# Attention and expert kernel: two dense blocks' activations ahead of the one-hot rows, first gates on their own, a loaded iota

## The chip, the cores and the metric

The kernel runs on one core of one Trainium2 chip. The metric is the device time of one execution in microseconds, as a median over executions. The engines of the core are called as the profile calls them: PE multiplies matrices (PEld are its weight loads), DVE, ACT and POOL work on vectors, SP issues most of the DMA transfers, and POOL issues the indirect ones. Each engine executes its own instructions in order and waits for the others by semaphores, so an instruction that waits holds up all that stand behind it on its engine. SP's queue is such an engine too.

## What is computed

The output is the input plus two branches, both over the normalized input `xn` (2048 rows, 512 columns):

```python
# attention: 32 heads of 16, one shared key and value head
q = (xn @ wq).reshape(...); k = xn @ wk; v = xn @ wv
p = softmax(q k^T * 16 ** -0.5); a = (p v) @ wo
# experts: 32 heads, each with two sets of 64 scores; 64 x 64 = 4096 experts
s1, s2 = q1 @ k1.T, q2 @ k2.T              # per row and head, 64 scores each
t1, i1 = top2(s1); t2, i2 = top2(s2)
top_s, top_e = top2(t1 + t2, over the 4 pairs)  # index = i1 * 64 + i2
g = softmax(top_s)
act = gelu(xn . u[top_e])                  # tanh form
b = sum over heads and both experts of g * act * v[top_e]
out = x + a + b
```

So each row has 64 experts out of 4096, two per head.

## The kernel before

**Groups and ways.** The 16 row tiles of 128 are four groups of four. For groups 0 and 1 the experts are *gathered*: for each row tile and slot, POOL fetches 128 rows of `u` and `v` by index (L880), DVE forms a dot product (L892, `dot`) and later adds the weighted `v` row to an accumulator (L927, `add`). For groups 2 and 3 they are computed *densely*: all 4096 experts, in 32 blocks of 128, are multiplied with the group's 512 rows, and a matrix of gates, zero nearly everywhere, selects. The sequence `SEQ` is: scores of group 0, two eighths of group 1, group 2 with its dense stage, the rest of group 1, group 3 with its dense stage.

**Attention goes on all the time.** `att_steps` (L1037) is called 280 times. 256 of them put out two key tiles' worth of attention: scores on PE (L318), an exp on ACT (L321, tile `pt`), and the product with the values on PE (`pv`, L332). In the middle of a step `mid` puts out expert work for DVE and ACT; at its end `fill` runs the generator `score_thread` (L998) for as much PE work as a linear plan (`aim`) allows. What the generator yields is the planned PE cost of the piece in us. A yield of `None` ends the filling of this step, so that the next piece comes behind another attention step.

**Lists of later work.** `ON_ACT`, `LAST` and `LATER` hold ACT work for the next `mid` or the one after it; `BEHIND` holds DVE work that is laced into the dots and adds of a `mid`; `STORES` holds DMA issues, run at the start of the next step. How many dots a step may put out is set by `pos`, which grows by 1.7, 2.5 or 1.4 slots per step according to `dense_on` (L1152), and over the last quarter evenly to the end. All engines are scheduled by hand here: the order of the calls is the order on the engines.

**From scores to gates.** `item` (L513) multiplies a row tile with an eighth of the score weights (`psc`, L532), and DVE finds the best values and their indices (MAX8 L542, FIND_INDEX8 L544). After four row tiles `batch` (L561) forms the pairs: two index rows `df1`, `df2` (L628, L629) and, after an exp on ACT that comes two `mid`s later, the gates `dgt` (L632 to L640, among them `gh` at L638). They are written to tiles named `da`. `dense` (L645) then does this:

1. It makes an iota of shape 128x128x16 on POOL (L701) and fetches the first two raw expert blocks (`rw`, 256 KB of `u` and 256 KB of `v` each, L654, two buffers).
2. It transposes the three rows (`ptd`, L711) into `tr`.
3. In 32 rounds of 16 columns it forms one-hot rows on DVE by comparing the iota with `tr` (`oh`, L722 to L725) and multiplies them on PE (`pg`, L749). ACT copies the products to `gst` (L754). Every fourth round two stores of 16 blocks each go to `d_g` in memory, in packets of 256 bytes (L757).
4. Behind the last store `first_gates` (L728) fetches the gate rows of blocks 0 and 1 back (`gy`, L672) and four tiles of `x`.
5. For each block (L788): `split` (L677) makes a high and a low part of `u` and `v` (cast on ACT L684, subtraction on DVE L685); 12 matmuls give the activations (`pact`, L796); square, tanh and products with the gate on ACT and DVE follow (L818 to L825); the result is split again into `wd` (L828, L832); and for two blocks at a time 24 matmuls (`pout`, L780) and four additions (L783) bring them to the accumulator. `fetch_gates` (L666) waits for a free gate tile.

`split` of a block, `fetch` of the block two further on and the fetch of its gates are queued as the loop goes on, so the raw blocks, the gate stores and the gate fetches share one SP queue with attention's loads (`qa`, `ot`, `rc`) and with the loads of partial sums (`fin`, L420) that finished row tiles need on DVE (L433).

Of the kernel before, what the change touches and what calls it, by code (L numbers as in the profile page):

```python
# [54 lines left out]
def tile_kernel(ctx, tc, x, wq, wkv, wo, wqT, kT, uv, ub, vb, out):  # L55
# [17 lines left out]
    d_w = [dram.tile([P, KC, 2, 512], F32, name=f"dw{c}") for c in range(NC)]  # L73
    d_g = dram.tile([NB, P, 512], F32, name="dg")
# [478 lines left out]
    DT = []  # L553
# [7 lines left out]
    def batch(ph, c, b):  # L561
# [52 lines left out]
        if c == 0:  # L614
            DT.clear()
            dense_tiles()
# [14 lines left out]
        def gates():  # L631
# [8 lines left out]
            stt(dgt[:, :, 1, w], gg, GS, gh, op0=OP.mult, op1=OP.subtract)  # L640

# [3 lines left out]
    def dense(DG, after):  # L645

        df1, df2, dgt = DT[:3]
# [12 lines left out]
        def gate_tile(b):  # L660
            if b not in gates:
                gy = late[0].tile([P, 2, 512], F32, name="gy", tag="gy", bufs=3)
                gates[b] = gy
            return gates[b]

        def fetch_gates(b):  # L666
            if b < NB and b not in fetched:
                if formed[0] < b - 2:

                    store(lambda: fetch_gates(b))  # L670
                    return
                nc.sync.dma_start(gate_tile(b)[:, 0, :], d_g[b])  # L672
                fetched.add(b)

        splits, halved = {}, set()

        def split(b):  # L677
            if b < NB:
                if b not in raws:
                    run(STORES)  # L680
                rw = raws.pop(b)
                us, vs = wk_tile(), wk_tile()
                for i, w in enumerate((us, vs)):
                    nc.scalar.copy(w[:, 0, :], rw[:, i, :])  # L684
                    behind(lambda w=w, i=i: nc.vector.tensor_tensor(out=w[:, 1, :], in0=rw[:, i, :], in1=w[:, 0, :],  # L685
                                                                    op=OP.subtract))
                behind(lambda: halved.add(b))
                splits[b] = us, vs
# [11 lines left out]
        io = kt(F16, (P, P, TB))  # L700
        nc.gpsimd.tensor_copy(io, iota_h[:, :, None].to_broadcast([P, P, TB]))  # L701
        fetch(0)
        fetch(1)
        yield None
        tr = kt(F16, (P, 3, 512))
        for n, src in enumerate((df1, df2, dgt)):
            if n == 2:
                yield None
            p = xtile("ptd")
            for j in range(GT):  # L710
                nc.tensor.transpose(p[:, j * P:(j + 1) * P], src[:, j].rearrange("p r s -> p (r s)"), ident)  # L711
            nc.scalar.copy(tr[:, n, :], p)
            yield 0.45
        dense_on[0] = 2
# [3 lines left out]
        def onehot(q):  # L718
            if q < NQ:
# [3 lines left out]
                ob = kt(F16, (P, NB, TB))  # L723
# [4 lines left out]
        def first_gates():  # L728

            fetch_gates(0)  # L730
            fetch_gates(1)
# [6 lines left out]

        onehot(0)
        onehot(1)  # L740
        for q in range(NQ):
# [10 lines left out]
            def copies(pv_=pv_, st=st, ql=ql, t0=t0):  # L752
                for hb in range(2):
                    nc.scalar.copy(st[hb][:, :, ql * TB:(ql + 1) * TB], pv_[:, 16 * hb:16 * hb + 16, :])  # L754
                if ql == 3:
                    for hb in range(2):
                        store(lambda hb=hb: nc.sync.dma_start(  # L757
                            d_g[16 * hb:16 * hb + 16, :, t0:t0 + 64].rearrange("b p t -> p b t"), st[hb]))
# [11 lines left out]
        def sums():  # L770
# [4 lines left out]
            for j in range(GT):  # L775
                p = xtile("pout")
                n = 0
                for wd, vs in ready:
                    for a, c in TERMS:
                        nc.tensor.matmul(p, wd[:, a, j * P:(j + 1) * P], vs[:, c, :], start=n == 0, stop=n == 5)  # L780
# [7 lines left out]
        for b in range(NB):  # L788
            if b not in halved:
                flush()  # L790
            us, vs = splits.pop(b)
            p = xtile("pact")
            n = 0
            for k in range(KC):
                for a, c in TERMS:
                    nc.tensor.matmul(p, us[:, a, k * P:(k + 1) * P], XT[DG][k][:, c, :],  # L796
                                     start=n == 0, stop=n == 11)
                    n += 1
                if k == 0:
                    store(lambda b=b: fetch_gates(b + 1) if b else None)  # L800
                    if b % 2 == 0:
                        later_split(b + 2)
                if k == KC - 1 and b == NB - 1 and after is not None:
                    wp_read(after, range(2))
                if b == NB - 1 and after is not None:
                    load_phase2_xt(SEQ[after][0], k)
                if k < KC - 1:
                    yield 3 * UNIT
            wd = late[0].tile([P, 2, 512], F32R, name="wd", tag="wd", bufs=4)

            if b > 1 and b not in fetched:
                if formed[0] < b - 2:
                    flush()
                run(STORES)
            gy = gate_tile(b) if b < 2 else gates[b]
            gates.pop(b - 1, None)
            g, y = gy[:, 0, :], gy[:, 1, :]
            nc.scalar.activation(y, p, AF.Square, scale=C_CUB ** 0.5)  # L818
            stt(y, y, C_IN, p, op0=OP.add, op1=OP.mult)

            def gated(g=g, p=p):
# [4 lines left out]

            def high(y=y, wd=wd):
                nc.scalar.copy(wd[:, 0, :], y)  # L828
                behind(lambda: low(y, wd))
# [429 lines left out]
```

## Time and profile before

| | us |
|---|---|
| median of 3 runs | 2010.13 |
| lowest and highest | 2004.77, 2011.43 |
| profiled execution | 2014.99 |
| its span in the trace | 2013.3 |
| PE busy, granted clock over the span | 1883.9, 0.967 |
| last `psc` of group 2 ends, first `pg` begins | 613.1, 635.4 |
| last `pg` of group 2 ends, first `pout` begins | 760.2, 800.6 |
| last `psc` of group 3 ends, first `pg` begins | 1455.4, 1476.9 |
| last `pg` of group 3 ends, first `pout` begins | 1577.8, 1645.5 |

All stage times are from the trace's timeline, counted from the start of the span. A row of the timeline is: start, length, engine, line, operation, output and inputs by the program's names, count; in brackets the idle time of the engine before it and what ended it. SPq rows are the times in which SP issues a transfer, not the transfer itself. The granted clock (PEclk) is the share of full speed at which PE was clocked; at 0.6 its matmuls take longer, while they still count as busy.

### The profile page before, as it was taken

To read this page: it belongs to the slowest core of one execution; us is meant where nothing else is said; L and a number is where in the kernel's file an instruction comes from. 1 tells how busy PE (TensorE), PEld (TensorE's weight loads), DVE (VectorE), ACT (ScalarE), POOL (GpSimd) and SP (SyncE) were. 2 spreads that over 40 slices of the span, in tenths; PEclk is the share of its full clock that TensorE was granted. 3 is DMA by queue.
4 is the path that set the end of the run, shared out by engine and by line. 5 is a ranking of instruction groups with operands and counts; after the bars stand their busy time and mean duration, and the time that the engine had idled before them with its cause. 6 is when DMAs were issued, how large, how long until landed. Compare 5 with 4: busy or idle time off the path is not lost.

```text
span 2013.3 us, 34723 instructions
## 1 busy us (share of the span) xinstructions
PE 1883.9 (94%) x10990; PEld 1004.4 (50%) x10990; DVE 1683.2 (84%) x6713; ACT 1291.2 (64%) x1804; POOL 573.2 (28%) x542
## 2 busy tenths in 40 slices
PE   6869989899998997999999999999979789999997
PEld 4634444455554443555555445555545345555552
DVE  7536778889999867999999779999999668999993
ACT  2236556655556787778777565555568567788873
POOL 2202223222223223334344222222223333333320
PEclk9989999999998998999999999999989899999999
DMA  7856778787764769788889868776659877888761
GB/s 264 297 191 227 266 246 273 269 285 254 241 226 129 224 194 298 241 281 263 276 293 319 324 236 257 262 259 221 205 139 248 275 253 262 260 277 259 264 209 63
DMA packets 239882, 494.79 MB, mean 246 GB/s; under 512 B 93380, under 2 KB 93380, under 8 KB 239692
## 3 DMA queue, kind: packets, MB, share of 16 engines
q0 software_dynamic: 73728, 268.47, 40.3%
q1 hardware_dynamic: 163960, 222.44, 33.7%
q10 hardware_dynamic: 2004, 1.61, 0.3%
q8 instruction: 88, 1.44, 0.3%
q14 instruction: 102, 0.84, 0.1%
HBM read 429.51 MB, written 57.64 MB: 242 GB/s over the span
## 4 chain that ended last, share of the span: by engine, by line
PE 58%; DVE 25%; DMA 5%; ACT 2%; issue 2%; SPq 1%; ACTq 0%; DVEq 0%
PE pv L332 16%; PE sc L318 12%; PE psc L532 9%; PE pout L780 9%; PE pact L796 8%; DVE i L544 6%; DVE xa L927 4%; DVE m L542 4%; DVE g L892 4%; DMA dg<-gst 2%; DVE oh L722 2%; PE pg L749 2%; PE pwo L427 1%; ACT pt L321 1%; PE pw L487 1%
## 5 line engine op out<-in xcount | busy, mean ns | idle before, releaser
L321 ACT ACTIVATE pt<-sc 128x1024 f32<-128x1024 f32 x1024 | 993.5, 1025 | 495.6 <-PE sc L318 436.7
L880 POOL DMA_INDIRECT g<-in_uv_dram,idx x512 | 556.4, 1087 | 1368.7 <-DVE xa L927 701.0
L332 PE MATMUL pv<-pt,vaug 128*32 128x512 f32 x4096 | 517.0, 623 | 0.0
L318 PE MATMUL sc<-qa,kaug 64*128 64x512 f32 x2048 | 392.4, 457 | 17.4 <-ACT pt L321 16.0
L532 PE MATMUL psc<-wk,xt 128*128 128x512 f32 x1536 | 386.3, 401 | 18.8 <-DVE i L544 13.2
L927 DVE SCALAR_TENSOR_TENSOR xa<-g,w,xa 128x512 f32<-128x512 f32 x512 | 371.5, 747 | 0.0
L532 PEld LDWEIGHTS psc<-wk,xt 128*128 128x128 f32 x1536 | 280.5, 189 | 118.8 <-issue 42.3
L892 DVE CUSTOM_DVE_ANT_0 g<-g,xa 128x512 f32<-128x512 f32 x512 | 336.7, 683 | 2.4 <-DMA g<-in_uv_dram,idx 2.2
L318 PEld LDWEIGHTS sc<-qa,kaug 64*128 64x128 f32 x2048 | 159.1, 188 | 340.1 <-ACT pt L321 209.0
L332 PEld LDWEIGHTS pv<-pt,vaug 128*32 128x32 f32 x4096 | 109.7, 112 | 259.8 <-issue 258.2
L796 PE MATMUL pact<-xt,wk 128*128 128x512 f32 x768 | 198.4, 404 | 11.3 <-DVE fin L433 5.4
L780 PE MATMUL pout<-wk,wd 128*128 128x512 f32 x768 | 197.4, 405 | 10.1 <-DVE wd L832 5.8
L544 DVE FIND_INDEX8 i<-m,psc 128x8 uint32<-128x64 f32 x1024 | 206.7, 223 | 0.0
L542 DVE MAX8 m<-psc 128x8 f32<-128x64 f32 x1024 | 146.6, 216 | 43.5 <-PE psc L532 36.3
L796 PEld LDWEIGHTS pact<-xt,wk 128*128 128x128 f32 x768 | 140.9, 190 | 62.3 <-issue 18.0
L780 PEld LDWEIGHTS pout<-wk,wd 128*128 128x128 f32 x768 | 141.9, 190 | 58.5 <-DVE wd L832 7.1
L783 DVE TENSOR_TENSOR da<-da,pout 128x512 f32<-128x512 f32 x128 | 83.1, 682 | 9.0 <-PE pout L780 8.6
L915 DVE SCALAR_TENSOR_TENSOR w<-gth,ga 128x4 f32<-128x4 f32 x128 | 20.4, 159 | 83.2 <-ACT gth L908 82.9
L685 DVE TENSOR_TENSOR wk<-rw,wk 128x512 fp32r<-128x512 f32 x128 | 85.0, 684 | 0.0
L722 DVE TENSOR_TENSOR oh<-oh 128x2048 f16<-128x2048 f16 x64 | 78.1, 1220 | 6.7 <-PE pg L749 6.7
L749 PE MATMUL pg<-oh 128*128 128x32 f16 x1024 | 73.6, 246 | 9.1 <-DVE oh L725 9.0
L749 PEld LDWEIGHTS <-oh 128*128 128x128 f16 x1024 | 69.3, 162 | 20.5 <-issue 12.7
(150 smaller groups left out, 1350.4 us busy)
## 6 DMA issues: line engine op xcount, KB each, us to landing
wk<-dw SPq DMA_DIRECT2D x96, 512.0 KB
wqt<-in_wqT_dram SPq DMA_DIRECT2D x32, 512.0 KB
dw<-wk SPq DMA_DIRECT2D x32, 512.0 KB
rw<-in_ub_dram SPq DMA_DIRECT2D x64, 256.0 KB
rw<-in_vb_dram SPq DMA_DIRECT2D x64, 256.0 KB
dg<-gst SPq DMA_DIRECT2D x32, 512.0 KB
gy<-dg SPq DMA_DIRECT2D x64, 256.0 KB
qa<-dqh SPq DMA_DIRECT2D x128, 64.0 KB
```

Of the source, the lines that this page charges most:

```text
L318: nc.tensor.matmul(p[:, b, :], kaug[o:o + 64, kc * P:(kc + 1) * P], QA[u][o:o + 64, i, :], start=True, stop=True)
L321: nc.scalar.activation(pt, p, AF.Exp, scale=SCALE)
L332: nc.tensor.matmul(PV[u][32 * j:32 * j + 32, :], vaug[:, kc, :], pt[:, b, :], start=kc == 0, stop=kc == 15)
L532: nc.tensor.matmul(p, XT[g][k][:, a, j * P:(j + 1) * P], WC[n_][k][:, bb, :], start=n == 0, stop=n == 11)
L542: nc.vector.max(m8[:, jb, s, :], p[:, s * E:(s + 1) * E])
L544: nc.vector.max_index(i8[:, jb, s, :], m8[:, jb, s, :], p[:, s * E:(s + 1) * E])
L749: nc.tensor.matmul(p[:, i * NB:(i + 1) * NB], oa[:, :, i], ob[:, :, i], start=True, stop=True)
L780: nc.tensor.matmul(p, wd[:, a, j * P:(j + 1) * P], vs[:, c, :], start=n == 0, stop=n == 5)
L796: nc.tensor.matmul(p, us[:, a, k * P:(k + 1) * P], XT[DG][k][:, c, :], start=n == 0, stop=n == 11)
L880: nc.gpsimd.indirect_dma_start(out=gt, out_offset=None, in_=uv, in_offset=bass.IndirectOffsetOnAxis(ap=IDX[ph, c, ti][:, s:s + 1], axis=0))
L892: nc.vector.tensor_tensor_reduce(u, u, XN[TPH * ph + ti], scale=1.0, scalar=0.0, op0=OP.mult, op1=OP.add, accum_out=a[:, i:i + 1])
L927: nc.vector.scalar_tensor_tensor(acc, v, w[:, i:i + 1], acc, op0=OP.mult, op1=OP.add)
```

## The change

- `dense` is started earlier. It yields 0.0 twice before its real work; `score_thread` takes these steps ahead of the last eighth's first and second item, so that the two raw blocks are fetched, and the `u` halves of blocks 0 and 1 split, while the scores still run.
- `first(b)` computes the activations of blocks 0 and 1 and begins their gelu: square and copy on ACT, then on DVE the inner polynomial, later tanh and (tanh + 1) times the activation. Block 0 comes ahead of the transposes, block 1 between the first and the second one-hot set. In the loop over the blocks these two are only multiplied with their gates (`scaled`) and split. Their `v` halves are split during the one-hot rounds; blocks 0 and 1 leave the loop's `pact` work.
- From the third item of the last eighth to the end of the transposes `dense_on` is 3: no new dots, and one add per step.
- The iota is made once at the start by ACT, stored to memory (`dio`, 512 KB) and loaded by SP in each dense stage.
- The last store of each group is cut into blocks 0 to 2, 3 to 15 and 16 to 31; directly behind the first piece the gate rows 0, 1 and 2 and the `x` tiles are fetched. Gate rows up to 3 no longer wait for formed blocks.
- The small one-hot operand lives in one tile of three slots instead of tiles of its own. The first products (`sums`) are taken at block 4, and some points where the filling ended (`yield None`) are gone or moved.

```diff
@@ zero_m
+        io = gtile(F16, (P, P, 16))
+        nc.scalar.copy(io, iota_h[:, :, None].to_broadcast([P, P, 16]))
+        nc.sync.dma_start(d_io, io)
@@ batch: gates
+            if c == NC - 1:
+                gated_all.append(True)
@@ dense
+        def half_split(b, i):
+            rw, w = raws[b], wk_tile()
+            nc.scalar.copy(w[:, 0, :], rw[:, i, :])
+            behind(lambda: nc.vector.tensor_tensor(out=w[:, 1, :], in0=rw[:, i, :], in1=w[:, 0, :], op=OP.subtract))
+            return w
...
-        io = kt(F16, (P, P, TB))
-        nc.gpsimd.tensor_copy(io, iota_h[:, :, None].to_broadcast([P, P, TB]))
         fetch(0)
         fetch(1)
-        yield None
-        tr = kt(F16, (P, 3, 512))
-        for n, src in enumerate((df1, df2, dgt)):
-            if n == 2:
-                yield None
...
+        yield 0.0
+        early = []
+        on_act(lambda: early.extend(half_split(b, 0) for b in range(2)))
+        yield 0.0
...
+        def first(b):
+            p = xtile("pact")
+            for k in activations(b, early[b], p):
+                if k < KC - 1:
+                    yield 3 * UNIT
+            g, y = gate_rows(b), hh[:, b, :]
+            nc.scalar.activation(y, p, AF.Square, scale=C_CUB ** 0.5)
+            nc.scalar.copy(g, p)
+            nc.vector.scalar_tensor_tensor(y, y, C_IN, p, op0=OP.add, op1=OP.mult)
+
+            def go():
+                nc.scalar.activation(y, y, AF.Tanh)
+                behind(lambda: nc.vector.scalar_tensor_tensor(y, y, 1.0, g, op0=OP.add, op1=OP.mult))
+
+            LATER.append(go)
+            yield 3 * UNIT
...
+        io = kt(F16, (P, P, TB))
+        nc.sync.dma_start(io, d_io)
+        tr = kt(F16, (P, 3, 512))
+        hh = kt(F32, (P, 2, 512))
+        yield from first(0)
+        for n in range(2):
+            spread(n)
             yield 0.45
+        while not gated_all:
+            yield None
+        spread(2)
+        yield 0.45
...
-            fetch_gates(0)
-            fetch_gates(1)
+            for b in range(3):
+                fetch_gates(b)
...
         onehot(0)
+        yield from first(1)
         onehot(1)
...
-                    for hb in range(2):
-                        store(lambda hb=hb: nc.sync.dma_start(
-                            d_g[16 * hb:16 * hb + 16, :, t0:t0 + 64].rearrange("b p t -> p b t"), st[hb]))
-                    if t0 == 448:
-                        store(first_gates)
+                    cut = (0, 3, 16, NB) if t0 == 448 else (0, 16, NB)
+                    for b0, b1 in zip(cut, cut[1:]):
+                        store(lambda b0=b0, b1=b1: nc.sync.dma_start(
+                            d_g[b0:b1, :, t0:t0 + 64].rearrange("b p t -> p b t"),
+                            st[b0 // 16][:, b0 % 16:b0 % 16 + b1 - b0, :]))
+                        if b0 == 0 and t0 == 448:
+                            store(first_gates)
...
-                later_split(q - NQ + 2)
+            if q in (NQ - 6, NQ - 2, NQ - 1):
+                later_split((NQ - 6, NQ - 2, NQ - 1).index(q))
@@ dense, loop over the blocks
+            def scaled(y=y, g=g):
+                stt(y, g, 1.0 / GS, y, op0=OP.mult, op1=OP.mult)
...
+            else:
+                LAST.append(lambda scaled=scaled, high=high: (behind(scaled), on_act(high)))
@@ score_thread
+            dn = None
+            if ph >= NSP and c == NC - 1:
+                dn = dense(ph, n + 1 if n + 1 < len(SEQ) else None)
+                yield next(dn)
             for ti in range(TPH):
+                if dn and ti == 1:
+                    yield next(dn)
+                if dn and ti == 2:
+                    dense_on[0] = 3
...
-                yield from dense(ph, n + 1 if n + 1 < len(SEQ) else None)
+                yield from dn
@@ steps
-                pos += 2.1 if len(IDX) < NC * TPH else (1.7, 2.5, 1.4)[dense_on[0]]
+                pos += 2.1 if len(IDX) < NC * TPH else (1.7, 2.5, 1.4, 0.0)[dense_on[0]]
...
+                if dense_on[0] == 3:
+                    sums = min(sums, 1)
```

More of the change, by code (lines that the diff above doesn't have):

```diff
@@ L615, in batch @@
             DT.clear()
+            gated_all.clear()
             dense_tiles()
@@ L680, in split @@
                     run(STORES)
[L681 to L686, printed above, removed]
+                us = half_split(b, 0) if b > 1 else None
+                splits[b] = us, half_split(b, 1)
                 behind(lambda: halved.add(b))
-                splits[b] = us, vs
+                raws.pop(b)
         def later_split(b):
@@ L788, in dense @@
         for b in range(NB):
[L789 to L808, printed above, removed]
@@ L816, in dense, with gated @@
+            vs = splits.pop(b)[1]
+            gy = gates[b]
             gates.pop(b - 1, None)
[L817 to L821, printed above, removed]
+            g, y = (gy[:, 0, :], gy[:, 1, :]) if b > 1 else (gy[:, b, :], hh[:, b, :])
+            def gated(g=g, p=None):
                 stt(g, g, 1.0 / GS, p, op0=OP.mult, op1=OP.mult)
```

95 lines of the change are left out of this document (61 added, 34 removed).

## The prediction

> **What bounds the kernel now.** First the busy shares on the page:
>
> ```profile
> PE 1883.9 (94%) x10990; PEld 1004.4 (50%) x10990; DVE 1683.2 (84%) x6713; ACT 1291.2 (64%) x1804; POOL 573.2 (28%) x542
> ```
>
> PE (TensorE) sets the time. From 820 to 1100 us it is busy 279.4 of 280 us, from 1660 to 1960 us 299.7 of 300, so there only less PE work could help. What can be won lies where PE stands still or its granted clock falls. Windows of 5 us show where (columns: window, length, busy us of PE, PEld, DVE, ACT, POOL with counts, granted clock, DMA share, GB/s):
>
> ```profile
> 620.00:625.00 5.00, 2.21 (x20) 1.15 (x12) 4.66 (x32) 0.59 (x1) 0.00 (x0) 1.00 0.12 26
> 625.00:630.00 5.00, 3.56 (x16) 1.17 (x20) 4.86 (x17) 4.94 (x8) 1.88 (x2) 0.60 0.46 120
> 785.00:790.00 5.00, 2.22 (x9) 1.26 (x8) 1.36 (x3) 0.62 (x1) 1.87 (x2) 0.98 1.02 398
> 790.00:795.00 5.00, 1.87 (x5) 1.16 (x4) 3.60 (x6) 3.46 (x5) 1.14 (x1) 0.50 0.96 351
> 1460.00:1465.00 5.00, 0.00 (x0) 0.00 (x0) 4.96 (x48) 1.46 (x2) 0.00 (x0) 0.72 0.01 2
> 1600.00:1605.00 5.00, 0.10 (x1) 0.10 (x1) 0.84 (x2) 0.00 (x0) 0.00 (x0) 0.72 0.77 257
> ```
>
> There are two holes in each dense group (groups 2 and 3): A, between the last scores and the first one-hot rows (DVE is full, PE waits), and B, between the last one-hot product and the first `pout` (the DMA share is near 1). The timeline tells what ends the waits:
>
> ```profile
> 1467.47 1.97 PE L711 MATMUL ptd<-ident,da 128*128 128x128 f32 x8 [8.81 <-DVE da L628]
> ...
> 1452.16 2.54 DVE L638 TENSOR_SCALAR gh<-gd 128x32 f16<-128x32 f32 x1
> 1452.75 1.90 POOL L701 COPY oh<-iota_h 128x2048 f16<-128x2048 f16 x1
> ...
> 764.53 8.32 SPq L757 DMA_DIRECT2D dg<-gst  x2
> 777.67 0.81 SPq L672 DMA_DIRECT2D gy<-dg  x2
> 780.72 0.43 SPq L654 DMA_DIRECT2D rw<-in_ub_dram  x1
> 788.70 0.62 ACT L684 CAST wk<-rw 128x512 fp32r<-128x512 f32 x1 [4.46 <-DMA rw<-in_ub_dram]
> 793.37 2.08 PE L796 MATMUL pact<-xt,wk 128*128 128x512 f32 x4 [3.13 <-DVE wk L685]
> ...
> 1604.16 0.69 DVE L433 TENSOR_TENSOR fin<-fin,pwo 128x512 f32<-128x512 f32 x1 [12.45 <-DMA fin<-dpart]
> ...
> 771.30 3.04 PE L796 MATMUL pact<-xt,wk 128*128 128x512 f32 x12
> ```
>
> In A, PE waits for the last batch of indices, which stands behind expert dots and adds on DVE. In B of group 2 the last two stores of the gate rows hold the SP queue 13.1 us (764.53 to 777.67); the first gates, and behind them the raw block that ACT needs next, come after. In B of group 3 the `fin` loads stand in the same queue, and DVE waits 12.45 us for one.
>
> To compare the orders of the two programs I price PE work at full clock: an attention step (8 scores, 16 `pv`) 3.24 us, twelve `pact` matmuls 3.0, sixteen `pg` 1.1, four `ptd` 0.6, eight `pwo` records 3.6, all from steady stretches. What a stretch takes above that is its excess:
> - last `psc` to first `pg`: group 2 22.3 us for 11.5 of work (excess 10.8); group 3 21.4 for 8.2 (13.2).
> - first to last `pg`: 124.8 for 111.7 (13.1); 101.0 for 87.4 (13.6).
> - last `pg` to first `pout`: 40.4 for 28.1 (12.3, and 2.4 right behind it); 67.7 for 52.3 (15.4, and 3.9 behind it).
>
> In all 84.7 us, the most that this change could touch.
>
> **The change part by part.**
>
> *Two activations in hole A.* Per group 24 `pact` matmuls (6.0 us) move from B to A, with two squares and tanhs (0.60 and 0.64 us), four more DVE operations (0.68) and one added ACT copy per block (0.6, hidden: ACT is 64% busy). While `dense_on` is 3 no dots are issued and one add at a time; hardly any DVE work lies between the last batch and the first one-hot.
> Group 2: the changed order puts block 0 and the first transposes behind the first attention step after the scores. PE is free at 616.2, `pact` ends at 619.2. On the way to the last batch DVE trades one dot (0.6) for two subtractions of the split (1.2), so the indices come at 624.1 instead of 623.5; PE waits 4.9 us. Then transposes, attention (about 5 us, the clock being low after the wait), transposes, block 1 and attention end at 638.5. In 25.4 us 17.4 of work is done: excess 8.0, gain 2.8. Bounds: 0 to 6.0 (both blocks wholly inside the hole).
> Group 3: three of the matmuls run before the attention step, nine behind it, until 1461.6. DVE saves the 2.36 us that `gh` L638 took above its 0.18 under the POOL copy, pays 1.2 for the subtractions and trades a dot for an add: indices at 1466.3 instead of 1467.4, PE waits 4.7 instead of 8.8. The gates come 6 us after the indices now; with the dots gone the exp on ACT sets that, some 5 us; block 1 then runs until 1476.6, when the first `pg` begins, and the second one-hot set, which stands behind block 1's DVE step, costs PE 2 us. Gain 13.2 - 7.0 - 2.0 = 4.2; bounds 0 to 9.
>
> *The clock after hole A.* It stays at 0.60 to 0.83 from 625 to 665 us, which makes up most of the 13.1; shorter waits should shorten that. Nothing in the trace shows how much: bounds 0 and 9 for both groups, I take 3, because waits as short as 2.35 and 1.76 us preceded the 0.60.
> [...]
>
> *The iota.* Two POOL copies (1.90) go; what they cost is in group 3 above, in group 2 no DVE row is longer beside it. In their place SP gets two loads of 512 KB; such a load (`wk<-dw`) is common, and it is issued behind the last scores, some 10 us ahead of its use: 0. The first two raw blocks are fetched about three items earlier, past `qa` and `rc` on SP; the DMA share is 0.02 to 0.67 from 600 to 620 us, which hides them: 0, and 2 us (their 1 MB at some 400 GB/s) if it did not.
>
> *Start.* One ACT copy of 128x2048 (by twice the 1.02 us of 128x1024: about 2 us) and a store of 512 KB in a part that is not PE-bound (ACT 3.6 of 10). It stands ahead of the `kaug` issues, in a gap of ACT of 3.3 us: I take +1, bounds -1 to +3.
>
> *First gates by themselves, hole B.* The last store is cut into blocks 0 to 2, 3 to 15 and 16 to 31, with the fetches of gates 0 to 2 and four `x` loads after the first piece. Two stores hold the queue 13.1 us; 3 of 32 blocks are 1.2 us of that, so gates 0 and 1 come some 10 us earlier. But behind the loads SP issues the other 29 blocks (12 us) and only then raw block 4 and gate 3. That order matters: ACT reaches block 4's cast at the second attention step after the last `pg`, because blocks 3 and 4 are split together, and its exps stand behind that cast; DVE meets `gated` of block 3, whose gate row has the same wait.
> Group 2, counted from the last `pg`: attention to 4, block 2 to 7, attention to 10.5, block 3 to 15; then PE waits. Bytes ahead of raw block 4 are those ahead of block 3 before (landed at 28.5), started 3 us sooner, one wait for a store's end shorter, one gate row more: about 25.5. Cast and subtraction: 27. At the low clock that follows, first `pout` at 36, for 18.6 of work: excess 17.4 and some 2 behind it, against 12.3 + 2.4 + 2 before: a loss of 2.5. Bounds: gain 6 (it lands with the first gates), loss 9 (all of 12 us of stores fully in front of it).
> Group 3: four `pwo` groups lie between, so block 3 is wanted only near 30, its raw block lands near 28; the cast waits some 6, and one `fin` load stands behind the stores too. Against stops of 5.4, 3.9 and 1.4 with their low clock I take 13 of excess for 19.3: gain 6; bounds loss 3 to gain 15.
>
> *Dots put off.* About 4 steps at 1.7 slots per group, 13 slots; dot and add stand 0.61 and 0.66 us apart in the timeline, so 17 us of DVE work go to the last quarter, where DVE is busy 274 of 300 us and PE is full. The 26 us of slack take it; I take +1 (bounds 0 to 4), for adds that come late to `pout`. Without that slack it would cost all 17.
>
> **The sum.** -2.8 - 4.2 - 3 + 1 + 2.5 - 6 + 1 = -11.5 us. The profiled execution took 2015.0 us (span 2013.3), so 2003.5; the median shown, 2010.1, is 4.9 below it: about 1999.
>
> **The rivals.**
> 1. *Hole B gives back what hole A won.* For it: the bytes in front of the next raw block are the same. Against: group 3 has other work there. B in both groups at +3 and no clock won: -7 + 6 + 2 = +1, about 2011.
> 2. *The split store becomes the stop: slower.* One mechanism: raw block 4 and gate 3 stand behind 12 us of small-packet stores and the new loads, while ACT and DVE ask for them a block earlier, so ACT, DVE and PE stop together in both groups. For it: the 4.46 us stop at the same cast. Against: `fin` waits go. Price: B +9 and +3, dots +4, against -7 in A: +9, about 2019. It decides once block 4 lands later than some 30 us after the last `pg`.
> 3. *More than I count.* `fin` no longer stops DVE and the clock stays up: B 0 and -15, A -7, clock -6: -28, 1982. For it: 12.45 us is the longest wait there is; against: `fin` is still behind the stores.
> 4. *The holes are only moved* (indices late, blocks wait with them): the 8.81 us wait is DVE's, and the 4.9 us left in group 2 is longer than the 2.35 there now. If only group 3's 4.2 is kept and B is even: 2006.
>
> **How the numbers follow.** Forecast 0.45, rivals 0.17, 0.14, 0.14, 0.10. What can be told from no change is 0.3%, 6 us: below 2004 or above 2016. Faster: 0.35 of the forecast's 0.45, rival 3, 0.03 of rival 1, 0.05 of rival 4: 0.57. Slower: 0.12 of rival 2, 0.03 of rival 1: 0.15. Same: 0.28. The forecast's own range is 1991 to 2008; to hold 8 in 10 it goes to 1981 and 2018, which takes in rival 3 and most of rival 2.
>
> **What would show it.** Hole A: `pact` records before the first `ptd`, waits there of 4 to 5 us instead of 8.81, no POOL copy, `gh` at 0.18. B: `gy<-dg` within 5 us of its store; then a long `rw` wait at ACT's cast and a low clock in group 2, shorter `fin` waits in group 3. Late: PE still full from 1660 on. I am wrong if ACT's wait for raw block 4 is absent or much over 16 us, or if PE shows gaps after 1660.

## The result and the profile after

The changed kernel takes 2021.11 us (median of 20 runs, 2013.13 to 2025.06), the kernel before in the same series 2014.08. The ratio is 1.0031, 95% interval [1.0016, 1.0047]: slower by about what can be told from no change. The forecast was 1999 us and the range ended at 2018. The forecast started from a median of 2010.13 us for the kernel before (3 runs); 20 runs give 2014.08, so 4 of the 22 us between forecast and result belong to that base. The profiled execution took 2022.62 us, its span is 2020.9 against 2013.3.

The busy shares on the page hardly differ from those before:

```profile
PE 1883.2 (93%) x10990; PEld 1002.7 (50%) x10990; DVE 1679.2 (83%) x6713; ACT 1295.8 (64%) x1809; POOL 571.0 (28%) x540
```

So the 7.6 us are places where PE stands. The timeline of hole A in both groups (line numbers are those of the changed kernel from here on: `ptd` L750, `pact` L725, `gh` L643):

```profile
616.04 3.01 PE L725 MATMUL pact<-xt,wk 128*128 128x512 f32 x12
622.95 0.65 PE L750 MATMUL ptd<-ident,da 128*128 128x128 f32 x4 [3.90 <-DVE da L633]
...
1459.12 0.18 DVE L643 TENSOR_SCALAR gh<-gd 128x32 f16<-128x32 f32 x1
1471.38 1.09 PE L750 MATMUL ptd<-ident,da 128*128 128x128 f32 x8 [2.66 <-DVE da L633]
```

The wait of 8.81 us is 2.66 now, `gh` has lost its 2.36 us, and `pact` stands ahead of the transposes. Last `psc` to first `pg` takes 23.7 us for 17.4 of work in group 2 and 18.4 for 14.2 in group 3: excess 6.4 and 4.2, where it was 10.8 and 13.2. Hole A is won.

The same view of hole B in group 2 (SPq rows are issues; the rest are ACT, DVE and PE behind them):

```profile
764.18 0.38 SPq L811 DMA_DIRECT2D dg<-gst  x1
769.71 1.28 SPq L682 DMA_DIRECT2D gy<-dg  x3
771.03 2.39 SPq L787 DMA_DIRECT2D da<-in_x_dram  x4
773.46 6.17 SPq L811 DMA_DIRECT2D dg<-gst  x2
779.73 2.67 SPq L660 DMA_DIRECT2D rw<-in_ub_dram  x1
...
774.96 0.73 PE L725 MATMUL pact<-xt,wk 128*128 128x512 f32 x2 [0.65 <-ACT wk L689]
787.10 0.62 ACT L689 CAST wk<-rw 128x512 fp32r<-128x512 f32 x1 [11.67 <-DMA rw<-in_ub_dram]
789.23 0.69 DVE L877 SCALAR_TENSOR_TENSOR gy<-gy 128x512 f32<-128x512 f32 x1 [8.95 <-ACT gy L894]
790.50 0.68 DVE L690 TENSOR_TENSOR wk<-rw,wk 128x512 fp32r<-128x512 f32 x1
791.24 5.51 PE L725 MATMUL pact<-xt,wk 128*128 128x512 f32 x16 [15.55 <-DVE wk L690]
805.54 4.64 PE L836 MATMUL pout<-wk,wd 128*128 128x512 f32 x10 [3.56 <-DVE wd L888]
```

The first piece is issued in 0.38 us, then SP stands 5.15 us until it has landed, because the gate rows that are fetched next are read from it. Only then come the gates, the `x` tiles, 6.17 us of the other two pieces, and raw block 4. ACT's wait at its cast is 11.67 us (4.46 before), PE's behind it 15.55 (3.13). What PE waits for is not block 4 but block 3: only two of its 12 `pact` matmuls run before the stop (774.96). Its raw rows were cast on ACT right before it (774.30), but the subtraction for it on DVE (790.50) stands behind a product that waits 8.95 us for a tanh (L894), and that tanh stands on ACT behind the cast of block 4.

In group 3 the two later pieces take 8.20 us of the queue, ACT waits 14.2 and PE 16.9. There all pieces also leave later. First the changed kernel, then the kernel before:

```profile
1610.62 0.38 SPq L811 DMA_DIRECT2D dg<-gst  x1
...
1582.68 8.30 SPq L757 DMA_DIRECT2D dg<-gst  x2
```

The first piece is issued 13.1 us after the end of the last `pg` (1610.62 less 1597.53), behind a `fin` store and load and eight `qa` loads; in the kernel before the two stores went out 4.9 us after it (1582.68 less 1577.83), ahead of these. Last `pg` to first `pout`, with the wait right behind it, has an excess of 23.2 us in group 2 (14.7 before) and 22.9 in group 3 (19.3 before).

A third place was not foreseen: the junction, where dense group 2 ends and the scores of group 1 go on. The timeline there:

```profile
1105.01 0.38 SPq L457 DMA_DIRECT2D out_dram<-fin  x1
1119.68 0.32 SPq L424 DMA_DIRECT2D fin<-dpart  x1
1126.63 5.36 SPq L509 DMA_DIRECT2D wk<-dw  x6
...
1124.45 0.69 DVE L456 TENSOR_TENSOR fin<-fin,xa 128x512 f32<-128x512 f32 x1 [5.73 <-DMA fin<-dpart]
1125.79 1.66 PE L836 MATMUL pout<-wk,wd 128*128 128x512 f32 x6 [1.87 <-DVE da L839]
1134.25 0.96 PE L536 MATMUL psc<-wk,xt 128*128 128x512 f32 x3 [2.23 <-DMA wk<-dw]
```

A finished row tile of the gathered groups is stored (`out`), and as there is one `fin` buffer the next `fin` load stands in SP's queue for that store, 14.65 us in the chain of waits. DVE waits 5.73 us for this load, PE for DVE's additions, and the score weights `wk` are issued 4.6 us later than before (1126.63 against 1121.99). PE's longer waits there are 1.87, 2.23 and 1.52 us, where the kernel before has one of 2.12, and from 1136.0 to 1142.7 us the granted clock is 0.50, where it stayed at 1.00 before. To measure it: the eight attention steps from step 128 to step 136 (step n is the exp 4n) hold the same PE work in every version; they take 65.4 us here and 58.6 before. The 3.5 us of added waits and an estimated 3.4 us lost at half clock (half of the 6.7 us at 0.50) make up these 6.8.

### The profile page after: what moved, and what is told of

Same layout as the page of the kernel before. It is cut to its first block, busy times and chain, and to the rows that moved or that the text cites. A ratio compares the mean times of both kernels' runs of the same rounds, so it can differ in the third digit from the quotient of the medians.

```text
span 2020.9 us, 34731 instructions
## 1 busy us (share of the span) xinstructions
PE 1883.2 (93%) x10990; PEld 1002.7 (50%) x10990; DVE 1679.2 (83%) x6713; ACT 1295.8 (64%) x1809; POOL 571.0 (28%) x540
## 4 chain that ended last, share of the span: by engine, by line
PE 61%; DVE 20%; DMA 5%; issue 4%; ACT 2%; POOL 1%; SPq 1%; DVEq 0%; ACTq 0%; POOLq 0%
PE pv L336 17%; PE sc L322 12%; PE psc L536 10%; PE pout L836 8%; PE pact L725 8%; DVE i L548 5%; DVE xa L982 3%; DVE m L546 3%; DVE g L947 3%; PE pg L802 2%; DMA out_dram<-fin 2%; PE pwo L431 1%; ACT pt L325 1%; PE pw L491 1%; DMA wk<-dw 1%
## 5 line engine op out<-in xcount | busy, mean ns | idle before, releaser
L725 PE MATMUL pact<-xt,wk 128*128 128x512 f32 x768 | 198.6, 403 | 18.9 <-DVE wk L690 15.6
L725 PEld LDWEIGHTS pact<-xt,wk 128*128 128x128 f32 x768 | 140.5, 189 | 69.5 <-issue 16.0
L836 PEld LDWEIGHTS pout<-wk,wd 128*128 128x128 f32 x768 | 142.1, 190 | 56.5 <-DVE wd L888 6.8
L689 ACT CAST wk<-rw 128x512 fp32r<-128x512 f32 x128 | 73.9, 628 | 27.3 <-DMA rw<-in_ub_dram 25.9
```

The costliest lines, as they stand in the source:

```text
L836: nc.tensor.matmul(p, wd[0][:, a, j * P:(j + 1) * P], vs[:, c, :], start=n == 0, stop=n == 5)
```

## The experiments

Every version but the kernel before and its three variants has the order of PE's instructions of the changed kernel, so stages can be compared by their length. Hole A is counted from the start of the last `psc` to the start of the first `pg`, hole B from the last `pg` to the first `pout`, in the one profiled execution of each run. Steps 56 to 104 take in the whole dense stage of group 2, steps 180 to 212 that of group 3, each with the same PE work in every version. All lengths in us; the ratio is to the kernel before, run beside it.

| run | median | ratio, 95% interval | A, groups 2, 3 | B, groups 2, 3 | steps 128 to 136 | steps 56 to 104, 180 to 212 |
|---|---|---|---|---|---|---|
| before | 2014.08 | 1 | 22.7, 21.8 | 40.4, 67.7 | 58.6 | 344.6, 241.1 |
| after | 2021.11 | 1.0031 [1.0016, 1.0047] | 24.1, 18.8 | 38.1, 60.9 | 65.4 | 346.3, 241.9 |
| e1_no_defer | 2025.75 | 1.0059 [1.0034, 1.0084] | 28.2, 23.1 | 41.1, 61.5 | 60.4 | 356.1, 243.3 |
| e2_raw_first | 2014.39 | 0.9999 [0.9975, 1.0023] | 25.2, 18.9 | 33.4, 59.0 | 65.1 | 345.1, 241.1 |
| e3_old_store | 2011.84 | 0.9993 [0.997, 1.0015] | 24.9, 19.9 | 38.0, 58.1 | 63.5 | 348.0, 242.1 |
| e4_pool_iota | 2020.25 | 1.0029 [1.0006, 1.0052] | 25.2, 19.7 | 38.5, 62.4 | 65.0 | 349.3, 237.4 |
| e5_pay_back | 2017.94 | 1.0012 [0.9985, 1.0038] | 25.1, 19.7 | 39.1, 60.0 | 64.4 | 349.1, 245.2 |
| e6_old_store_pay_back | 2009.92 | 0.9986 [0.996, 1.0013] | 24.2, 19.7 | 36.0, 56.5 | 64.6 | 343.6, 231.5 |
| e9_old_store_no_defer | 2017.49 | 1.0035 [1.0011, 1.0059] | 26.1, 22.8 | 33.3, 57.8 | 64.1 | 354.6, 239.3 |
| e10_relief | 2005.95 | 0.997 [0.9948, 0.9992] | 25.1, 20.0 | 37.8, 56.5 | 56.7 | 347.3, 240.0 |
| e12_relief_cut | 2012.13 | 1.0003 [0.9981, 1.0026] | 24.9, 19.7 | 38.7, 62.5 | 56.4 | 345.5, 241.7 |
| variants of before: e7_cut_only | 2011.81 | 1.0013 [0.9985, 1.0041] | 21.1, 22.3 | 49.0, 66.8 | 61.2 | 347.2, 246.8 |
| e8_defer_only | 2010.31 | 0.9997 [0.9973, 1.0021] | 18.8, 18.9 | 39.6, 72.1 | 65.3 | 337.7, 241.9 |
| e11_defer_relief | 2006.12 | 0.9976 [0.9948, 1.0004] | 17.9, 18.1 | 37.4, 69.4 | 56.8 | 333.2, 246.5 |

Each run of an experiment has 12 timed executions, which spread by 8 to 21 us. The intervals of two ratios reach some 0.0025 to each side, so one pair alone does not tell apart what differs by less than about 7 us (0.0035 of 2012); the verdicts below rest on pairs that agree and on the stages. Each stage length is from one execution, and not always a typical one: those of e3 and e5 were the slowest of their 12, that of e7 (2026.20 us) the second slowest.

**Without the put-off dots (e1_no_defer).**

```diff
                 if dn and ti == 2:
-                    dense_on[0] = 3
+                    dense_on[0] = 0
```

> The changed kernel without the one step that puts the dots off: during the scores of a dense group's last columns the gathered slots' dots keep their usual rate of 1.7 a step. Theory J (the junction behind dense group 2 costs 7 us because the gathered groups turn over 22 us later there, so the store of fin, its reload and the six wk loads stand one behind the other in SP's queue): the first fin loads lie near 1031 to 1090 again instead of 1053 to 1120, the 14.65 us wait of the next fin load for the store before it falls under 6, the exp count loses its jump of +7 between steps 132 and 136, hole A gives back 2 to 4 us in each group because the dots are in DVE's way again; the time is 2014 to 2018, some 5 us under the changed kernel's 2021. Rival D (the jump follows from the dense group's own later end, whatever the dots do): the jump stays and the time is 2021 to 2025.

The junction behaves as theory J said (60.4 us in place of 65.4), but the time rises to 2025.75, above the ranges of J and D. Hole A gets 4 us longer in both groups: PE waits 4.5 and 2.3 us at the transposes of group 2 where it waited 3.9 and 0.8. Without it the excess of hole A is 10.4 us in group 2 and 8.5 in group 3: the kernel before has 10.8 and 13.2, the changed kernel 6.4 and 4.2. So the put-off is nearly all that the change gains in hole A of group 2 and half of it in group 3, and the junction is what it costs. By the ratios it is worth 0.0028 of the time here and 0.0042 with the old store (e9 against e3). What I took for a harmless side step is its best part.

**The order of the last stores (e2_raw_first, e3_old_store).**

```diff
+        late_store = lambda f: behind(lambda: store(f))
-                        store(lambda b0=b0, b1=b1: nc.sync.dma_start(
+                        (late_store if b0 and t0 == 448 else store)(lambda b0=b0, b1=b1: nc.sync.dma_start(
```

> The changed kernel with the second and third piece of the last gate store put behind the next raw blocks' fetches in SP's queue (in group 2 block 4, in group 3 blocks 3 and 4), nothing else moved. Theory S (hole B's stop is SP's queue: the raw block is late because the two pieces, 6.2 us in group 2 and 8.2 us in group 3, are issued ahead of it): the ACT cast's wait for the raw block falls from 11.7 to 4 to 6 us in group 2 and from 14.2 to 5 to 8 in group 3, the last-pg-to-first-pout stage gets 5 us shorter in group 2 and 5 to 7 in group 3, the time is 2009 to 2013. Rival G (block 3's gates, now stored later, take the raw block's place as the stop): ACT waits less, but DVE waits for gy<-dg by as much, the stage stays within 2 us and the time within 2019 to 2022. Rival L (the packets of the store share the transfer engines with the raw block): the wait falls by under 3 us and the time is 2017 to 2020.

```diff
-                    cut = (0, 3, 16, NB) if t0 == 448 else (0, 16, NB)
+                    cut = (0, 16, NB)
...
-                        if b0 == 0 and t0 == 448:
+                        if b0 == 16 and t0 == 448:
```

> The changed kernel with the last gate store in two pieces again (16 and 16 blocks) and the first three gates and the x loads behind both, as in the kernel before. Theory S (the stop in hole B is at raw block 4, and the cut only serves the first gates, which are not what is late): the raw block is issued at about the same time as in the changed kernel, the ACT wait stays at 10 to 15 us, the first gates come some 6 us later and show in the products of blocks 0 and 1; the time is 2020 to 2024. Rival C (the cut itself, with its extra issue and 3-block packets, is what the hole costs): hole B's stage gets 4 us or more shorter in each group and the time is under 2014.

With the raw block first, ACT's wait falls from 11.67 to 2.90 us (9.7 in group 3), hole B gets 4.7 and 1.9 us shorter, and the time goes from 1.0031 to 0.9999 of before. Theory S is right about the place, too hopeful about group 3 (9.7 for 5 to 8, 1.9 for 5 to 7) and a little about the time. But with the old store the time falls as far, and there S had expected no gain: by the time rival C holds, the cut itself costs. C's 4 us or more in each hole B did not come. The timeline of SP in e3_old_store, with ACT behind it:

```profile
765.91 6.15 SPq L811 DMA_DIRECT2D dg<-gst  x2
773.98 1.31 SPq L682 DMA_DIRECT2D gy<-dg  x3
775.34 2.52 SPq L787 DMA_DIRECT2D da<-in_x_dram  x4
777.95 0.39 SPq L660 DMA_DIRECT2D rw<-in_ub_dram  x1
...
787.06 0.62 ACT L689 CAST wk<-rw 128x512 fp32r<-128x512 f32 x1 [8.13 <-DMA rw<-in_ub_dram]
```

Both pieces are issued in one go, and 1.9 us after the second SP goes on with the gates: the landing of the first piece is hidden behind the issue of the second. From the store to the raw block's issue it is 12.0 us; in the changed kernel it is 15.6, because the small piece's landing (5.15 us) stands ahead of the others' issue (6.17) instead of beside it. The gates come 8.1 us after the store in place of 5.5, which costs less than the raw block's delay. The profiled execution of e3 (2021.25 us) was the slowest of its 12, so its stages say less than its median: hole B is 0.1 and 2.8 us shorter. Over the versions with the put-off dots that have the cut (after, e4, e5, e12) the cast of the late raw block begins on average 24.2 us after the end of the last `pg` in group 2 and 38.6 in group 3, with the old store (e3, e6, e10) 22.2 and 34.7.

In both kernels SP itself stands for the landing before it goes on with the gates: 5.1 us by its waits for the 96 KB of the changed kernel's first piece, 4.7 us for the two stores of the kernel before. In the changed kernel the DMA share was 1.01 from 764 to 768 us and 0.22 from 768 to 770.

**The iota on GpSimd again (e4_pool_iota).**

```diff
-        nc.sync.dma_start(io, d_io)
+        nc.gpsimd.tensor_copy(io, iota_h[:, :, None].to_broadcast([P, P, TB]))
```

> The changed kernel with the iota written by GpSimd again instead of being loaded, at the place where the load stands. My prediction's price for the load was nothing, with a bound of 4 us a group for the slow gate arithmetic (gh at some 3 us beside the GpSimd copy in the kernel before, 0.18 without it). Theory Z (the copy now runs beside the early activations' stage, where DVE has slack): time within 2 us of the changed kernel's 2021. Rival P (the clash is back on the path of the gates): the PE wait at the last ptd rises from 2.7 to 3.9 us to 6 to 9 in both groups and the time is 2025 to 2029.

1.0029 against 1.0031, `gh` takes 0.18 us here too: theory Z, the load is worth nothing by itself. The PE waits at the `ptd` stay at 3.9 and 2.7 us, so rival P falls. At its new place the copy no longer meets the gate arithmetic (copy at 1468.15, `gh` at 1462.95).

**Paying the dots back (e5_pay_back, e6_old_store_pay_back).**

```diff
-(1.7, 2.5, 1.4, 0.0)[dense_on[0]]
+(1.7, 2.7, 1.4, 0.0)[dense_on[0]]
```

> The changed kernel with the put-off dots paid back during the dense blocks: 2.7 slots a step in place of 2.5 there, which puts the last fin, xa and wk issues behind dense group 2 back into the kernel before's order in SP's queue. Theory J (the junction's loss is that order: fin's store, the next fin load and the wk loads one behind the other): the exp count's jump between steps 132 and 136 falls from +6.9 to between 0 and +2, the dense steps keep their 6.95 us, since 0.2 slots a step is some 0.25 us of DVE against the 5% that it has free there, and the time is 2013 to 2017. Rival V (DVE has no room in the dense blocks): the steps there get longer, 3 us or more in all before step 132, and the time stays at 2018 to 2023. Rival K (the jump comes from the clock and the late wk slots, not from the order): the jump stays at 5 to 7.

> The changed kernel with both repairs: the last gate store in two pieces again with the first gates behind both, and 2.7 slots a step in the dense blocks. The two pieces' issue (6.2 us) and their landing overlap, where the changed kernel has SP's queue stand 5.5 us for the small store's landing and then issues 6.2 us more. If both theories hold and add (old store some 7 us by its median, the junction some 5): 2004 to 2009, under the kernel before's 2014. If the old store's gain was the luck of its runs, it comes out where the run with the pay-back alone does, within 2 us.

SP's order behind group 2 is that of before again, PE's waits for `wk<-dw` are gone, and the eight steps still take 64.4 and 64.6 us: theory J falls as the whole explanation, and the jump of 6.0 and 6.1 us is the one that rival K named. The timeline of e6_old_store_pay_back at the junction:

```profile
1109.80 0.36 DVE L374 RECIPROCAL rc<-rc 128x32 f32<-128x32 f32 x1 [3.12 <-DMA rc<-dsum]
1113.77 0.69 DVE L947 CUSTOM_DVE_ANT_0 g<-g,xa 128x512 f32<-128x512 f32 x1 [2.44 <-DMA xa<-dxn]
...
1117.20 0.98 PE L836 MATMUL pout<-wk,wd 128*128 128x512 f32 x3 [2.14 <-DVE wd L888]
1121.73 5.51 PE L836 MATMUL pout<-wk,wd 128*128 128x512 f32 x13 [3.55 <-DVE wd L888]
```

The stop has moved from SP to DVE: attention's `rc` stands 3.12 us for its load (2.68 in the kernel before) and a dot of the next gathered tile 2.44 us for its `xa` load, the last `wd` tiles of the group stand behind it, and PE waits 5.7 us for them. So what the junction does not bear is DVE being late there, whatever makes it late. e6 has both repairs and comes to 0.9986 (2009.92 us, just above its range), e5 alone to 1.0012: the old store gains again.

**One part of the change on the kernel before (e7_cut_only, e8_defer_only).** The first has only the cut store with the first gates behind its first piece, the second only `dense_on` 3 during the last scores, with 2.6 slots a step in the dense blocks.

> The kernel before with one part of the change alone: the last gate store in three pieces (3, 13 and 16 blocks) and the first gates and x loads behind the first piece. Theory C (the cut serialises: SP's queue stands for the small store's landing, then issues the rest, so the raw blocks behind it come 4 to 8 us later): the raw block behind it waits 4 to 8 us longer than before in both groups and the time is 2016 to 2022. Rival E (the cut hurts only where two early blocks make ACT ask for raw block 4 sooner): the first gates come 6 us earlier, nothing else is late, and the time is 2010 to 2014.

> The kernel before with another part alone: the dots put off during the last scores, and 2.6 slots a step in the dense blocks to pay them back. Theory H (what shortens hole A is a free DVE, not the early activations): the PE wait at the transposes of ptd falls from 2.4 to under 1.5 us in group 2 and from 8.8 to under 5 in group 3, and the time is 2006 to 2011. Rival W (PE has no other work in hole A, so the gates' own chain sets it): the waits move by under 2 us in both groups and the time is 2013 to 2017.

By their times neither can be told from the kernel before; the medians lie in the ranges of rival E and theory H. The cut shows in the place: ACT's wait for the raw block in group 2 is 11.8 us where the kernel before has 4.46, 7.3 more, as theory C said, and hole B is 49.0 us for 40.4; in group 3, where C had expected the same, it costs nothing. The put-off shortens hole A by 3.9 and 2.9 us; the waits at the transposes are 1.7 and 6.8 us, nearer to rival W than to theory H. From step 56 to step 128, which takes in the whole of group 2's stage, it is 6.9 us ahead of the kernel before, and the junction takes 6.7 back (65.3 for 58.6).

**The early activations without the put-off (e9_old_store_no_defer): both diffs of e1 and e3.**

> The changed kernel with the old two-piece store and without the put-off dots: what is left of the change are the early activations, the early raw blocks and gates, and the loaded iota. Theory D (the put-off dots are what pays in hole A of group 2, some 8 to 10 us, and what costs some 5 at the junction; the early activations alone fill PE but not DVE): hole A is 28 us long in group 2 and 23 in group 3 as in the run without the put-off alone (24 and 19 with it), the jump at the junction is 0 to 3, and the time is 2014 to 2020, no better than the kernel before. Rival A (the early activations pay by themselves, 4 to 8 us): 2005 to 2011.

2017.49, theory D; rival A falls. Two numbers of D are misses: hole A of group 2 is 26.1 us long and not 28, and the junction takes 64.1 us though nothing was put off, with 4.8 us of waits for `wd`. The junction is a narrow place for any version, not for the put-off alone.

**Relief at the junction (e10_relief, e11_defer_relief, e12_relief_cut).** Four blocks before the dense group ends, the rate goes down to 1.7 slots; e10 has the old store, e12 the cut, e11 is e8 with the relief.

```diff
         for b in range(NB):
+            if b == NB - 4:
+                dense_on[0] = 0
```

> The changed kernel with the old two-piece store, 2.7 slots a step in the dense blocks, and 1.7 a step from block 28 on. Theory W (behind dense group 2 PE waits for DVE's last wd tiles, 5.7 us in the run with both repairs, because DVE still has paid-back dots there, one of them standing 2.4 us for its xa load, and the clock falls to half behind the wait): with four slots, some 5 us of DVE, less there the wait falls under 3 us, the jump between steps 132 and 136 from 6 to 0 to 2, and the time to 2003 to 2007. Rival Q (the wait is set by the xa load and the order in SP's queue and not by DVE's load): the jump stays at 4 to 7 and the time at 2008 to 2012.

> The kernel before with the put-off dots, 2.6 slots a step in the dense blocks and 1.7 from block 28 on, no early activations and no loaded iota. If theory W holds, the jump falls from 6.7 to 0 to 2 and the time from 2010 to 2003 to 2006. Beside the changed kernel with the same repairs it prices the early activations: if they pay, this run is 3 us or more slower than that one; if they only move the hole, the two agree within 3 us.

> The changed kernel with the cut store as it is, 2.7 slots a step in the dense blocks and 1.7 from block 28 on. It differs from the run with the relief and the old store in the cut alone. Theory C (the cut costs by the landing that SP's queue waits for): 4 to 8 us slower than that run, hole B longer by 2 us in group 2 and 3 in group 3. Rival N (the medians' difference between cut and old store so far was their spread): the two agree within 2 us.

The eight steps take 56.4 to 56.8 us in all three, less than in the kernel before. In all three PE is busy 51.86 of the 52 us from 1096 to 1148, at a clock of 1.00, and in e10 DVE's waits there are for PE and ACT (2.8 us the longest), none for a transfer. Windows of 5 us at the junction, first of the changed kernel, then of e10_relief (columns as in the windows above: PE first, the granted clock third from the end):

```profile
1120.00:1125.00 5.00, 3.92 (x28) 1.27 (x26) 0.55 (x1) 3.15 (x4) 0.00 (x0) 1.00 0.85 272
1130.00:1135.00 5.00, 2.77 (x23) 0.93 (x14) 3.74 (x8) 3.34 (x5) 2.19 (x3) 1.00 1.04 413
1135.00:1140.00 5.00, 3.48 (x9) 2.62 (x9) 1.61 (x14) 0.00 (x0) 1.52 (x2) 0.59 1.03 410
```

```profile
1120.00:1125.00 5.00, 5.00 (x33) 2.45 (x33) 2.00 (x5) 3.73 (x4) 0.94 (x1) 1.00 1.03 313
1130.00:1135.00 5.00, 5.00 (x29) 3.23 (x31) 3.78 (x32) 1.81 (x3) 0.00 (x0) 1.00 0.78 313
1135.00:1140.00 5.00, 5.00 (x27) 1.95 (x20) 5.00 (x26) 3.93 (x6) 1.07 (x1) 1.00 0.07 15
```

PE has no gap and keeps its clock; in the changed kernel the clock is 0.59 in the window behind the waits. Theory W holds in its numbers. The relief moves the row tiles' turnover as well as DVE's load, so which of the two frees DVE stays open.

Two prices follow. The cut: e12 is 6.2 us slower than e10, with hole B 0.9 and 6.0 us longer. Five pairs differ in the cut alone: e12 and e10 by 0.0033 of the time, after and e3 by 0.0038, e5 and e6 by 0.0026, e1 and e9 by 0.0024, e7 and the kernel before by 0.0013. All have the same sign; their mean is 0.0027, 5.4 us. Over the four cut versions named above hole B is 38.6 and 61.5 us on average, over the three with the old store 37.3 and 57.0, which makes 5.8.

The early activations: e10 and e11 differ by 0.2 us, e6 and e8 by 0.4. Beside the put-off they are worth nothing that can be told. Without it, e9 against the kernel before, they cost with all that came with them 0.0035 [0.0011, 0.0059]. The steps say where. Group 2 takes 344.6 and 347.2 us in the kernel before and e7, 337.7 and 333.2 with the put-off (e8, e11). It takes 354.6 and 356.1 with the early activations alone (e9, e1), and 343.6 to 349.3 in the eight versions with both. So in group 2 the put-off wins some 10 us and the early activations, with what came with them, lose as much; in group 3 they win some 4 us on average, 240.3 for 244.1, inside the spread of the runs. The 6 us left over do not show in the medians, and one execution of each version does not tell why. e10_relief beats the kernel before, 0.997 [0.9948, 0.9992], and by the two ratios it lies 0.6% under the changed kernel; e11 is as fast without them, though its interval just reaches 1.

## Why the prediction was wrong

- *Two activations in hole A*, -2.8 and -4.2: won 4.4 and 9.0, the waits 3.90 and 2.66 us for 4.9 and 4.7. Without the put-off the early activations win 0.4 and 4.7 (e1). The size was off because the put-off dots' gain was not a term of its own: without them hole A is 4.1 and 1.2 us longer in group 2 (e1 against after, e9 against e3) and 4.3 and 2.9 in group 3.
- *The clock after hole A*, -3: between first and last `pg` the excess fell by 4.7 in group 2 and rose by 6.8 in group 3 (117.9 us for 97.5 of work). The second number is mostly no property of the change: with the same order of PE's instructions this stage took 112.0 (e6) to 121.7 us (e5), and with that of the kernel before 101.0 to 107.6 (e7), for some 10 us less work.
- *The iota*, 0: right (e4). *Start*, +1: the first attention exp comes 1.8 us earlier; over all versions it lies 0.1 to 4.0 us earlier, with the iota's copy and without, so this says nothing.
- *First gates by themselves, hole B*, +2.5 and -6: measured +8.5 and +3.6. This is the step that failed, most of all in group 3, where "its raw block lands near 28; the cast waits some 6". The cast began 39.2 us after the last `pg` (1636.69 less 1597.53) and waited 14.2. The runs put three things in its place.
  - The price of the cut. I took the 13.1 us of the two stores as if they went by blocks, "3 of 32 blocks are 1.2 us of that". But they are 8.3 us of issue and 4.7 in which SP stands for the landing. The small piece holds the queue for 5.5 us (0.38 and 5.15), and the rest is then issued behind it. That costs some 5 us of the whole time.
  - SP's order in group 3. I had only "one `fin` load" behind the stores; in fact a `fin` load and eight `qa` loads stand ahead of them, and the first piece is issued 8.2 us later behind the last `pg` than the stores before. With the old store the cast still begins at 34.7 us on average, so the cut is only some 4 of the 11 us by which 28 was missed. No run moves the stores ahead of the `qa` loads, so that the late issue makes up the rest is not shown.
  - The cost in group 2. There the landing was forecast well (25.5, the cast came at 23.9). But I had "block 3 to 15" done before PE's wait, and block 3 stands in that wait with ten of its 12 matmuls, by way of ACT's tanh and DVE's subtraction. So hole B stays 38.1 us long (40.4 before) though it holds some 10 us less of PE work.
- *Dots put off*, +1, bounds 0 to 4: +6.8 at the junction. I let the 13 slots go to the last quarter. But each later dot also moves the gathered tiles' turnover, with its `out`, `fin` and `xa` transfers, onto the end of dense group 2, where DVE has `wd` to deliver. The last stretch, which I had named as the risk, stayed full: 298.2 of 300 us from 1660 to 1960.

The terms measured, -4.4 - 9.0 - 4.7 + 6.8 + 8.5 + 3.6 + 6.8, make +7.6 us, and the span is 7.6 longer. That they meet so well is luck: by the steps the 7.6 are -1.2 up to step 56, +1.7 in group 2, +6.8 at the junction, -1.6 up to step 180, +0.9 in group 3 and +1.0 behind it. So group 2 came out 2.3 us worse than its three terms, and smaller pieces took that back. Rival 2, at 2019, is what happened, with its prices of +9 and +3 in hole B and +4 for the dots; it had 0.14. Its condition (block 4 later than 30 us after the last `pg`) was met in group 3 alone.

## What to carry to other kernels

The store that was cut so that its head could be read back early made the issuing queue stand 5.15 us for the head's landing: let the rest's issue (6.17 us) cover that time, or put what others need next ahead of it. Work put off on an engine that is over 90% busy (DVE from 1080 to 1120 us: 35.9 of 40 us before, 36.5 after) came back here: the junction took 65.4 us with it and 60.4 without (e1). Look up what such work triggers where it lands, and make room there. Filling one hole with work taken from the next one won little here, where the second hole is a wait for a transfer (ACT's 11.67 us for the raw block): 10 us of PE work left hole B of group 2, and it became 2.3 us shorter.

## What was not expected of the hardware

The clock fell without a long gap. In group 3 of the changed kernel PE's last waits before 1488 are 0.88 and 0.41 us, and from there to 1513 us the clock swings between 0.50 and 1.00 while PE shows as busy. The same window in the changed kernel and in e4_pool_iota, which has the same PE instructions in the same order and comes to them some 4.6 us later:

```profile
1500.00:1510.00 10.00, 10.00 (x83) 4.91 (x84) 6.54 (x13) 7.41 (x14) 0.27 (x1) 0.73 0.27 55
```

```profile
1500.00:1510.00 10.00, 10.00 (x110) 5.95 (x108) 8.92 (x20) 9.24 (x15) 0.00 (x0) 1.00 0.52 107
```

The two waits do not decide it: e4_pool_iota has them too, 0.89 and 0.41 us at 1490.74 and 1491.65, and keeps 1.00. Nor does one longer wait. After 2.66 us in hole A of group 3 the clock stayed at 1.00 in the changed kernel; in e4_pool_iota the same wait of 2.66 us ended at 1475.22, and then:

```profile
1476.00:1478.00 2.00, 2.00 (x11) 0.77 (x13) 1.79 (x3) 1.85 (x3) 0.96 (x1) 0.57 0.09 12
```

After 3.55 us at the junction of e6 it was 0.50. So the length of one wait does not tell what the clock does behind it: 0.50 came behind 3.55 us, 0.57 and 1.00 behind 2.66, 0.50 and 1.00 behind 0.88 and 0.41. No run here isolates the cause.
